# Projecting eight narrow main tiles and four 32-row strips in one go, in place of three groups on the full TensorE array

## The chip, the cores and the metric

One core of a Trainium2 chip. The metric is device microseconds (us) of one execution.

## The reference, cut to what matters

```python
B, T, D, K = (2, 16000, 144, 15)          # x: B,T,D   w: K,D,2D   w_o: D,D   all bf16
# h = causal convolution of x with 15 taps, dilation 2
f = h[..., :D].copy()
g = h[..., D:].copy()
z = jnp.tanh(f) * _sigmoid(g)
return z @ w_o
```

The last line, `z @ w_o`, is the projection. D is 144, which is 16 more than the 128 rows of the TensorE array. The change is about how those 16 are carried.

## The kernel before, as far as the change touches it

The 32,000 positions are cut into 128 segments, one for each row of the array, and time is handled in "octets": eight consecutive time steps of all 128 segments. The z of an octet has 8 x 144 = 1152 columns. One DMA transposes it into nine blocks of 128 rows, `ZT[:, zt, 0..8, :]`, each of which is the stationary operand of matmuls with w_o as the moving one. In the kernel before, the 1152 columns lie in their natural order, so most blocks hold the end of one time step and the start of the next. Blocks inside a group therefore need w_o shifted and padded with zeros for two steps (288 columns), those at a group's border for one (144 columns):

```python
GROUPS = ((0, 3), (3, 6), (6, 8))

def project(o, gi, last=False):
    a, c = GROUPS[gi]
    ...
    bk = _Bank()                                   # one PSUM bank a group
    for blk in range(a, c + 1):
        q0, q1 = max(blk - 1, a), min(blk, c - 1)
        wi = 2 * blk - 1 if q0 == blk - 1 else 2 * blk
        def f(t, q0=q0, n=q1 - q0 + 1, ...):
            c0 = bk.b * 512 + (q0 - a) * D
            return t.matmul(PS[:, c0:c0 + n * D], lhsT=ZT[:, zt, blk, :], rhs=WOR[:, wi:wi + n, :]..., start=first, ...)
        fns.append(f)
    g.add("pe", fns, r=[("ZT", zt)] + wor_keys, alloc=[bk], ...)
    # ... ScalarE evicts the bank to OS, which frees it (L847); the third group also stores OS
```

The convolution is done in 30 units, as sums of products in pairs of banks; a unit makes half of the time steps of two octets, so that on average one octet is projected in a unit. Three small pieces matter here. "Ya" (weights `WV`, two matmuls) fills one bank of a pair, and ScalarE copies that bank to the other one of the pair. "Yb" (`WD,DD`, four matmuls) then adds to both. "Xa" (`WT,DU`, two matmuls) fills the first bank of another pair, for which two banks must be free. All other large items are sums of four to eight matmuls; the "D" items, of which `D11` comes first (`WA,DD`), add to banks that VectorE has prepared.

```python
def copy(bk):      # L898 before, L924 after
    g.add("act", lambda e: e.activation(bank(bk.b + 1), bank(bk.b), ACT.Copy), w=[bk], ...)
def item_Ya(u):
    s["Y", 0] = _pair()
    shared(s["Y", 0], V..., V..., WV[:, 0, :], WV[:, 1, :], ...)   # two matmuls
    copy(s["Y", 0])
def item_Xa(u, k):
    s["X", k] = _pair()
    shared(s["X", k], DU..., DU..., WT..., WT..., ...)             # two matmuls
    copy(s["X", k])
def item_Yb(u):    # four matmuls into both banks of s["Y", 0]
    ...
    g.add("pe", fns, r=keys, w=[s["Y", 0]], dur=4 * MM)
```

The order of a unit on TensorE is a string that a list scheduler follows (O0, O1, O2 are the three groups of the projection; a plus sign marks work of the next unit or the one after it, begun early):

```python
PATTERN = "Y0a O2+ X0a+ O1+ Y0b X0b+ D11 D00 S0+ X1a+ D10 Y01 S1+ X1b+ D01 VE+ VF+ O0+"
```

After the D items, `finish` makes tanh and sigmoid on ScalarE into TS and one multiply of 288 columns on VectorE into Z.

## Time and profile before

| | before |
|---|---|
| time, median of 2 (lowest, highest) | 322.32 us (322.23, 322.41) |
| span of the profiled core | 320.3 us |
| one unit in the steady stretch | 9.37 us |
| TensorE, VectorE, ScalarE busy | 313.1, 282.5, 269.6 us |
| projection of an octet, start to start | 0.98 us |

TensorE is the engine that the others wait for, so the unit's 9.37 us is a sum of TensorE's steps. The shown durations of matmuls overlap (the last of a run is shown 0.16 us beyond its step), so steps are read from one start to the next. The lines that carry this are in the prediction below. One more is wanted for comparison later, from the waits of the kernel before; it gives an instruction, what released it, the total in us, how often, and the longest:

```profile
PEld PS L740 <- ACT PS L925: 4.3, 23, 0.4
```

It is a small wait that the kernel before already has, about 0.2 us of the weight loads' time in most units, for ScalarE's copy of the sum "S1".

### The profile page before, as it was taken

The page shows a single profiled execution, that of the slowest core. Times are in us where ns is not written, and L with a number is a line of the kernel's source. Part 1 is how long each engine was busy: PE and PEld are TensorE (multiplying, and loading weights), DVE is VectorE, ACT ScalarE, POOL GpSimd, SP SyncE. Part 2 cuts the span into 40 slices and gives each one's busy share as a digit, 9 for nine tenths or more (in the row PEclk, how much of TensorE's full clock was granted, in tenths as well). Part 3 has the DMA queues.
Part 4 walks back from the last instruction along what each step waited for, and adds up shares of the span by engine and source line. Part 5 has one row for each costly group of instructions (what it writes and reads, how often), then busy time and mean ns, then how long its engine had stood idle before and what let it go on. Part 6 is the DMA issues. An engine that isn't in the chain of part 4 may idle for free.

```text
span 320.3 us, 6963 instructions
## 1 busy us (share of the span) xinstructions
PE 313.1 (98%) x2670; PEld 243.4 (76%) x2670; DVE 282.5 (88%) x610; ACT 269.6 (84%) x636; POOL 16.9 (5%) x29
## 2 busy tenths in 40 slices
PE   7999999999999999999999999999999999999994
PEld 6877777777777777777777777777777777777674
DVE  2999989898998989899898989989898998884774
ACT  3898789889797988979798897979889797778674
POOL 8109100000000000000000000000000000000000
PEclk9999999999999999999999999999999999999999
DMA  8799994939599494978959398894949377131653
GB/s 211 228 225 202 239 194 91 202 92 207 157 145 234 86 230 103 188 171 103 281 84 242 96 200 155 141 248 77 224 120 193 89 144 170 48 69 70 113 128 96
DMA packets 127822, 50.40 MB, mean 157 GB/s; under 512 B 119134, under 2 KB 121615, under 8 KB 127789
## 3 DMA queue, kind: packets, MB, share of 16 engines
q1 hardware_dynamic: 127273, 49.62, 74.7%
q0 software_dynamic: 512, 0.33, 0.5%
q8 instruction: 21, 0.34, 0.4%
q14 instruction: 12, 0.10, 0.1%
q10 hardware_dynamic: 4, 0.01, 0.0%
HBM read 11.82 MB, written 9.22 MB: 66 GB/s over the span
## 4 chain that ended last, share of the span: by engine, by line
PE 89%; ACT 5%; DVE 2%; DMA 2%; issue 1%; POOL 0%; ACTq 0%; POOLq 0%
PE PS L740 77%; PE PS L839 9%; DMA XA<-STA 2%; PE PS L548 1%; ACT STA L652 1%; ACT STB L672 1%; ACT XA L581 1%; DVE Xp L1019 0%; ACT XB L613 0%; PE PS L572 0%; DVE DD L692 0%; ACT TS L764 0%; PE PS L870 0%; PE PS L797 0%; ACT OS L847 0%
## 5 line engine op out<-in xcount | busy, mean ns | idle before, releaser
L1019 DVE TENSOR_TENSOR Xp<-PS,UX 128x576 f32<-128x576 f32 x90 | 62.9, 751 | 19.6 <-PE PS L740 19.3
L740 PE MATMUL PS<-WB,XB 128*128 128x288 bf16 x260 | 71.9, 286 | 0.0
L1031 DVE TENSOR_TENSOR PS<-PS,Xp 128x576 f32<-128x576 f32 x90 | 68.4, 760 | 2.1 <-ACT OS L847 1.0
L740 PE MATMUL PS<-WA,GD 128*128 128x288 bf16 x360 | 69.9, 286 | 0.0
L761 ACT ACTIVATE TS<-PS 128x288 f16<-128x288 f32 x125 | 51.7, 413 | 12.2 <-PE PS L740 11.2
L847 ACT ACTIVATE OS<-PS 128x432 bf16<-128x432 f32 (+1 forms) x88 | 42.3, 488 | 13.7 <-PE PS L839 12.8
L764 ACT ACTIVATE TS<-PS 128x288 f16<-128x288 f32 x125 | 51.4, 412 | 0.0
L672 ACT ACTIVATE STB<-XBc 128x768 bf16<-128x768 bf16 x60 | 50.8, 854 | 0.5 <-DVE XBc L639 0.5
L898 ACT ACTIVATE PS<-PS 128x288 f32<-128x288 f32 x120 | 46.2, 407 | 2.6 <-PE PS L740 2.4
L967 ACT ACTIVATE UX<-PS 128x576 f32<-128x576 f32 x60 | 39.2, 654 | 10.4 <-PE PS L740 10.1
L740 PE MATMUL PS<-WS,GU 128*128 128x288 bf16 x210 | 44.3, 287 | 0.0
L839 PE MATMUL PS<-WOR,ZT 128*128 128x144 bf16 (+1 forms) x322 | 42.4, 253 | 0.0
L740 PEld LDWEIGHTS PS<-WA,GD 128*128 128x128 bf16 x360 | 34.6, 98 | 9.8 <-DVE PS L1031 0.9
L769 DVE TENSOR_TENSOR Z<-TS 128x288 bf16<-128x288 f16 x125 | 37.1, 301 | 4.3 <-ACT TS L764 4.0
L740 PE MATMUL PS<-WC,XB 128*128 128x288 bf16 x120 | 34.3, 286 | 0.0
L839 PEld LDWEIGHTS PS<-WOR,ZT 128*128 128x128 bf16 x322 | 27.9, 98 | 6.3 <-ACT OS L847 0.5
L740 PE MATMUL PS<-WD,DD 128*128 128x288 bf16 x180 | 31.9, 286 | 0.5 <-ACT PS L898 0.5
L740 PE MATMUL PS<-WC,V 128*128 128x288 bf16 x180 | 30.6, 286 | 0.0
L740 PE MATMUL PS<-WA,DD 128*128 128x288 bf16 x180 | 30.6, 286 | 0.0
L740 PEld LDWEIGHTS PS<-WB,XB 128*128 128x128 bf16 x260 | 25.4, 98 | 6.4
L740 PE MATMUL PS<-WT,DU 128*128 128x288 bf16 x120 | 24.5, 286 | 0.1
L740 PEld LDWEIGHTS PS<-WS,GU 128*128 128x128 bf16 x210 | 18.5, 98 | 7.5 <-ACT PS L898 0.3
(82 smaller groups left out, 468.6 us busy)
## 6 DMA issues: line engine op xcount, KB each, us to landing
Xr<-in_x_dram SPq DMA_DIRECT2D x15, 576.0 KB, 4.6
out_dram<-OS SPq DMA_DIRECT2D x30, 288.0 KB, 3.0
WA<-in_w_dram SPq DMA_DIRECT2D x3, 288.0 KB, 5.3
ZT<-Z SPq DMA_TRANSPOSE x32, 3.7
Xp<-in_x_dram SPq DMA_DIRECT2D x2, 252.0 KB, 5.4
XA<-STA SPq DMA_TRANSPOSE x30, 3.5
XB<-STB SPq DMA_TRANSPOSE x30, 4.8
Xp<-in_x_dram SPq DMA_DIRECT2D x1, 441.0 KB, 4.3
```

Source lines behind the costliest of these rows:

```text
L548: g.add("pe", [lambda t: t.matmul(PS[:, BANK_O * 512:BANK_O * 512 + 128], lhsT=ID[:], rhs=ONES[:], start=True, stop=True)] * n, r=["ID", " ...
L672: return v.activation(STB[:, q, 6 * h:6 * h + 6, :], src, ACT.Copy)
L740: return lambda t: t.matmul(bank(bk.b), lhsT=lhs(), rhs=rhs(), start=start, stop=True, skip_group_check=True)
L761: return a.activation(TS[:, s, 0, :, :], both(bk, 0, D), ACT.Tanh)
L764: return a.activation(TS[:, s, 1, :, :], both(bk, D, D), ACT.Sigmoid)
L769: return v.tensor_tensor(dst, TS[:, s, 0, :, :], TS[:, s, 1, :, :], ALU.mult)
L839: return t.matmul(PS[:, c0:c0 + n * D], lhsT=ZT[:, zt, blk, :], rhs=WOR[:, wi:wi + n, :].rearrange("p a b -> p (a b)"), start=first, stop= ...
L847: return e.tensor_copy(dst, src) if eng == "dve" else e.activation(dst, src, ACT.Copy)
L898: g.add("act", lambda e: e.activation(bank(bk.b + 1), bank(bk.b), ACT.Copy), w=[bk], dur=t_act(N2), prio=0)
L967: g.add("act", lambda e: e.activation(UX[:, k, u % NU, :, :], both(X, 0, N2), ACT.Copy), r=[X], w=[("UX", k, u % NU)], frees=[X], dur=t_ac ...
L1019: g.add("dve", lambda v, k=k, wi=wi, vb=vb, us=us: v.tensor_tensor(wslot(wi), both(vb, 0, N2), UX[:, k, us, :, :], ALU.add), r=[vb, ("UX", ...
L1031: return v.tensor_tensor(both(d, 0, N2), src, wslot(wi), ALU.add)
```

## The change

The intent is to save TensorE time. The 16 channels left over from each time step are put together in the ninth block: two steps fill 32 rows. Four matmuls of 288 columns, each on its own strip of 32 rows of the array, then run side by side, while the other 128 channels of each step are one matmul of 144 columns on the full array. The core of the diff, with cuts marked by dots:

```diff
-        GROUPS = ((0, 3), (3, 6), (6, 8))
-        def project(o, gi, last=False):
+        def project(o, last=False):
             zt, os_ = o % NZT, oslot(o)
-            bk = _Bank()
+            pairs = [_pair(), _pair()] if o >= 0 else [_pair()]
...
+            def main(t, q):
+                c0 = (bk_of(q // 2).b + q // 2 % 2) * 512 + q % 2 * D
+                return t.matmul(PS[:, c0:c0 + D], lhsT=ZT[:, zt, q, :], rhs=WOM[:], start=q % 2 == 0, ...)
+            def rest(t, b, r0, n):
+                c0 = (bk_of(b).b + b % 2) * 512
+                return t.matmul(PS[:, c0:c0 + 2 * D], lhsT=ZT[r0:r0 + n, zt, 8, :],
+                                rhs=WOX[r0:r0 + n, 2 * b:2 * b + 2, :]..., start=False, ...)
+            if o >= 0:
+                fns = [lambda t, q=q: main(t, q) for q in range(8)] + [lambda t, b=b: rest(t, b, 32 * b, 32) for b in range(4)]
+                dur, out = 4 * MM + MM + SWITCH, [(pairs[0], 0, 4), (pairs[1], 4, 8)]
...
+            for pb, a, c in out:       # two evictions of two banks (576 columns) each, L874
+                def ev(e, ...): ...
-    PATTERN = "Y0a O2+ X0a+ O1+ Y0b X0b+ D11 D00 S0+ X1a+ D10 Y01 S1+ X1b+ D01 VE+ VF+ O0+"
+    PATTERN = "O1 Y0a X0a+ Y0b D11 X0b+ D00 S0+ X1a+ D10 Y01 S1+ X1b+ D01 VE+ VF+"
```

Besides this: w_o is loaded in 9 DMAs and not 16; two D items' gates are multiplied together in two VectorE instructions of 512 and 64 columns (L791) and not two of 288; TS has six slots and not four; the orders of the first and last units were retuned; and in a middle unit, as the two last lines of the diff show, D11 now stands directly behind Yb and ahead of X0b, where it stood behind X0b. `SWITCH` is 0.2 us, the author's allowance for turning the array to strips and back, which only the scheduler uses.

More of the change, by code (lines that the diff above doesn't have):

```diff
@@ L361, in _conv_wavenet_kernel @@
     NO = 3
-    NTS = 4
+    NTS = 6
     NST = 2
@@ L369, in _conv_wavenet_kernel @@
     LAG = 2
-    PATTERNS = {29: 'O2 O1 Y01 Y0a D11 O0 Y0b D01 D00 D10', 28: 'Y0a X0a+ O1+ Y0b X0b+ O2+ D11 S0+ D10 X1a+ D00 Y01 S1+ X1b+ VE+ O0+ D01 VF+', 1: 'Y0a O2+ X0a+ Y0b X0b+ D11 X1a+ O1+ D00 S0+ D10 Y01 S1+ X1b+ D01 VE+ VF+ O0+', 0: 'Y0a X0a+ Y0b D11 X0b+ D00 X1a+ O2+ O1+ O0+ S0+ D10 Y01 S1+ X1b+ D01 VE+ VF+', 2: 'Y0a O2+ X0a+ O1+ Y0b X0b+ D11 D00 S0+ X1a+ D10 Y01 S1+ X1b+ D01 VE+ O0+ VF+'}
+    SWITCH = 0.2
+    PATTERNS = {29: 'O1 Y01 Y0a D11 Y0b D01 D00 D10', 28: 'X0a+ Y0a O1 Y0b X0b+ D11 S0+ D10 X1a+ D00 Y01 S1+ X1b+ VE+ D01 VF+', 1: 'Y0a O1 X0a+ Y0b X0b+ D11 X1a+ D00 S0+ D10 Y01 S1+ X1b+ D01 VE+ VF+', 0: 'Y0a O1 X0a+ X0b+ Y0b D11 D00 X1a+ S0+ D10 Y01 S1+ X1b+ D01 VE+ VF+', 2: 'O1 Y0a X0a+ Y0b D11 X0b+ D00 X1a+ S0+ D10 Y01 S1+ X1b+ D01 VE+ VF+', 27: 'O1 Y0a D11 X0a+ Y0b S0+ X0b+ D00 X1a+ D10 Y01 S1+ X1b+ D01 VE+ VF+'}
     EARLY = 4
     EARLYC = 1
-    SPREAD = 12
+    SPREAD = 11
     SPREAS = 9
-    PATTERN = "Y0a O2+ X0a+ O1+ Y0b X0b+ D11 D00 S0+ X1a+ D10 Y01 S1+ X1b+ D01 VE+ VF+ O0+"
+    PATTERN = "O1 Y0a X0a+ Y0b D11 X0b+ D00 S0+ X1a+ D10 Y01 S1+ X1b+ D01 VE+ VF+"
     with contextlib.ExitStack() as st:
@@ L397, in _conv_wavenet_kernel @@
         WB = sb("WB", [NP, 3, N2], BF16)
-        WOR = sb("WOR", [NP, 16, D], BF16)
+        WOM = sb("WOM", [NP, D], BF16)
+        WOX = sb("WOX", [NP, 8, D], BF16)
         ONES = sb("ONES", [NP, NP], BF16)
@@ L528, in _conv_wavenet_kernel @@
         g.add("pool", lambda p: p.memset(XBc[:, 4:6, MB - 1, :], 0.0), w=["XBcz"], dur=0.2)
-        g.add("pool", lambda p: p.memset(Z[:], 0.0), w=[("Z", i, d) for i in range(NZ) for d in range(8)], dur=1.2)
-        g.add("pool", lambda p: p.memset(WOR[:], 0.0), w=["WORz"], dur=1.9)
+        g.add("pool", lambda p: p.memset(Z[:], 0.0), w=[(k, i, d) for k in ("Z", "Zr") for i in range(NZ) for d in range(8)], dur=1.2)
+        g.add("pool", lambda p: p.memset(WOX[:], 0.0), w=["WORz"], dur=1.0)
         g.add("sp", ld_wb(0), w=[("WB", 0)], dur=0.5, dma="wb", nbytes=73728)
@@ L754, in zslot, with finish @@
             return (o + 2 if o > 2 * LASTP and dl % 2 else o) % NZ
-        def finish(bk, z0, z1):
+        half_done = []
+        def finish(bk, z0, z1, mode=0):
+            if mode == 1 and ts_n[0] % 2:
+                ts_n[0] += 1
             s = ts_n[0] % NTS
@@ L765, in finish, with gt @@
             op = g.add("act", [th, sg], r=[bk], w=[("TS", s)], frees=[bk], dur=2 * t_act(2 * D), prio=0)
-            def gt(v):
-                dst = bass.AP(Z[:].tensor, (z0[0] * 8 + z0[1]) * D, [[NZ * 8 * D, NP], [((z1[0] - z0[0]) * 8 + z1[1] - z0[1]) * D, 2], [1, D]])
-                return v.tensor_tensor(dst, TS[:, s, 0, :, :], TS[:, s, 1, :, :], ALU.mult)
-            g.add("dve", gt, r=[("TS", s)], w=[("Z",) + z0, ("Z",) + z1], dur=t_tt(2 * D))
+            if mode == 1:
+                half_done.append((s, z0, z1))
+                return op
+            if mode == 3:
+                def gt(v):
+                    dst = bass.AP(Z[:].tensor, z0[0] * 8 * D + (z0[1] - 1) * DA, [[NZ * 8 * D, NP], [(z1[0] - z0[0]) * 8 * D, 2], [1, D]])
+                    return v.tensor_tensor(dst, TS[:, s, 0, :, :], TS[:, s, 1, :, :], ALU.mult)
+                g.add("dve", gt, r=[("TS", s)], w=[("Z",) + z for z in (z0, z1)] + [("Z", z[0], z[1] - 1) for z in (z0, z1)], dur=t_tt(2 * D))
+                return op
+            sets = [(s, z0, z1)]
+            if mode == 2:
+                sets.insert(0, half_done.pop())
+                assert sets[0][0] == s - 1 and sets[0][1][0] == z0[0] and sets[0][2][0] == z1[0]
+            n, s0, a0, a1 = len(sets), sets[0][0], sets[0][1], sets[0][2]
+            dd = z0[1] - a0[1]
+            for c0, base, w in ((0, 0, DA), (DA, 8 * DA, DB)):
+                def gt(v, c0=c0, base=base, w=w):
+                    dst = bass.AP(Z[:].tensor, a0[0] * 8 * D + base + a0[1] * w, [[NZ * 8 * D, NP], [dd * w, n], [(a1[0] - a0[0]) * 8 * D + (a1[1] - a0[1]) * w, 2], [1, w]])
+                    src = [bass.AP(TS[:].tensor, s0 * 4 * D + q * 2 * D + c0, [[NTS * 4 * D, NP], [4 * D, n], [D, 2], [1, w]]) for q in range(2)]
+                    return v.tensor_tensor(dst, src[0], src[1], ALU.mult)
+                g.add("dve", gt, r=[("TS", x[0]) for x in sets], w=[("Z" if c0 == 0 else "Zr",) + z for x in sets for z in x[1:]], dur=t_tt(2 * n * w))
             return op
-        wor_keys = [("WORp", dl, part) for dl in range(8) for part in range(2)]
+        wor_keys = [("WOR", dl) for dl in range(-1, 8)]
         tl_n = [0]
@@ L786, in ship_pair @@
             fns = []
-            for c0, bk in ((dl * D - 112, pa), (dl * D + DB, pb)):
+            for c0, bk in (((dl - 1) * DA, pa), (dl * DA, pb)):
                 for i in range(2):
@@ L796, in ship_pair @@
                 for k in range(2):
-                    fns.append(lambda t, i=i, k=k: t.matmul(PS[:, bo.b * 512 + i * D:bo.b * 512 + i * D + D], lhsT=zt(q, 256 * k + 128 * i, 128), rhs=WOR[:, 14 + k, :],
+                    fns.append(lambda t, i=i, k=k: t.matmul(PS[:, bo.b * 512 + i * D:bo.b * 512 + i * D + D], lhsT=zt(q, 256 * k + 128 * i, 128), rhs=WOM[:] if k == 0 else WOX[:, 0, :],
                                                             start=(i == 0 and k == 0), stop=True, skip_group_check=True))
@@ L821, in ship @@
             d0 = 6 if o < 0 else 0
-            g.add("sp", lambda e: e.dma_start_transpose(ZT[:, zt, d0:9, :], Z[:, z, d0 * 128:9 * 128]), r=[("Z", z, d) for d in dls],
+            g.add("sp", lambda e: e.dma_start_transpose(ZT[:, zt, d0:9, :], Z[:, z, d0 * 128:9 * 128]), r=[(k, z, d) for k in ("Z", "Zr") for d in dls],
                   w=[("ZT", zt)], dur=1.3, dma="zt", nbytes=(9 - d0) * 32768, soft=(xb2,))
-        GROUPS = ((0, 3), (3, 6), (6, 8))
-        def project(o, gi, last=False):
-            a, c = GROUPS[gi]
-            assert o >= 0 or gi == 2
+        def project(o, last=False):
@@ L830, in project @@
             zt, os_ = o % NZT, oslot(o)
-            bk = _Bank()
+            pairs = [_pair(), _pair()] if o >= 0 else [_pair()]
+            bk_of = lambda b: pairs[b // 2 if o >= 0 else 0]
             fns = []
-            for blk in range(a, c + 1):
-                q0, q1 = max(blk - 1, a), min(blk, c - 1)
-                wi = 2 * blk - 1 if q0 == blk - 1 else 2 * blk
-                def f(t, q0=q0, n=q1 - q0 + 1, blk=blk, wi=wi, first=(blk == a)):
-                    c0 = bk.b * 512 + (q0 - a) * D
-                    return t.matmul(PS[:, c0:c0 + n * D], lhsT=ZT[:, zt, blk, :], rhs=WOR[:, wi:wi + n, :].rearrange("p a b -> p (a b)"),
-                                    start=first, stop=True, skip_group_check=True)
-                fns.append(f)
@@ L842, in project @@
-            g.add("pe", fns, r=[("ZT", zt)] + wor_keys, alloc=[bk], dur=0.1255 + 0.1227 * (c - a - 1), floating=last, prio=3 if last else 1)
-            eng = "dve" if last else "act"
-            def ev(e):
-                dst, src = OS[:, os_, a:c, :].rearrange("p e d -> p (e d)"), PS[:, bk.b * 512:bk.b * 512 + (c - a) * D]
-                return e.tensor_copy(dst, src) if eng == "dve" else e.activation(dst, src, ACT.Copy)
-            op = g.add(eng, ev,
-                       r=[bk], w=[("OS", os_, d) for d in range(a, c)], frees=[bk], dur=t_ps((c - a) * D) if last else t_act((c - a) * D), prio=2 if last else 1)
@@ L850, in project @@
-            if os_ in last_store:
-                op.deps.add(last_store[os_])
-            if gi == 2:
-                projected.add(o)
-                d0 = 6 if o < 0 else 0
-                def stf(e):
-                    dst = bass.AP(out_t, (KD + 8 * o + d0) * D, [[L * D, NP], [1, (8 - d0) * D]])
-                    return e.dma_start(dst, OS[:, os_, d0:8, :].rearrange("p e d -> p (e d)"))
-                last_store[os_] = g.add("sp", stf, r=[("OS", os_, d) for d in range(d0, 8)], w=[], dur=0.5, dma="st", nbytes=NP * (8 - d0) * D * 2)
+            def main(t, q):
+                c0 = (bk_of(q // 2).b + q // 2 % 2) * 512 + q % 2 * D
+                return t.matmul(PS[:, c0:c0 + D], lhsT=ZT[:, zt, q, :], rhs=WOM[:], start=q % 2 == 0, stop=True, skip_group_check=True)
@@ new lines, in rest @@
+            def rest(t, b, r0, n):
+                c0 = (bk_of(b).b + b % 2) * 512
+                return t.matmul(PS[:, c0:c0 + 2 * D], lhsT=ZT[r0:r0 + n, zt, 8, :], rhs=WOX[r0:r0 + n, 2 * b:2 * b + 2, :].rearrange("p a b -> p (a b)"),
+                                start=False, stop=True, skip_group_check=True)
+            if o >= 0:
+                fns = [lambda t, q=q: main(t, q) for q in range(8)] + [lambda t, b=b: rest(t, b, 32 * b, 32) for b in range(4)]
+                dur, out = 4 * MM + MM + SWITCH, [(pairs[0], 0, 4), (pairs[1], 4, 8)]
+            else:
+                fns = [lambda t, q=q: main(t, q) for q in (6, 7)] + [lambda t: rest(t, 3, 0, NP)]
+                dur, out = 2 * MM, [(pairs[0], 6, 8)]
@@ new lines, in project, with ev @@
+            g.add("pe", fns, r=[("ZT", zt)] + wor_keys, alloc=pairs, dur=dur, floating=last, prio=3 if last else 1)
+            eng = "dve" if last else "act"
+            for pb, a, c in out:
+                def ev(e, pb=pb, a=a, c=c):
+                    nb = (c - a) // 2
+                    dst = OS[:, os_, a:c, :].rearrange("p (b e) d -> p b (e d)", b=nb)
+                    src = bass.AP(PS[:].tensor, (pb.b + a % 4 // 2) * 512, [[8 * 512, NP], [512, nb], [1, 2 * D]])
+                    return e.tensor_copy(dst, src) if eng == "dve" else e.activation(dst, src, ACT.Copy)
+                op = g.add(eng, ev, r=[pb], w=[("OS", os_, d) for d in range(a, c)], frees=[pb],
+                           dur=t_ps((c - a) * D) if last else t_act((c - a) * D), prio=2 if last else 1)
+                if os_ in last_store:
+                    op.deps.add(last_store[os_])
@@ L861, in project_some, with stf @@
+            projected.add(o)
+            d0 = 6 if o < 0 else 0
+            def stf(e):
+                dst = bass.AP(out_t, (KD + 8 * o + d0) * D, [[L * D, NP], [1, (8 - d0) * D]])
+                return e.dma_start(dst, OS[:, os_, d0:8, :].rearrange("p e d -> p (e d)"))
+            last_store[os_] = g.add("sp", stf, r=[("OS", os_, d) for d in range(d0, 8)], w=[], dur=0.5, dma="st", nbytes=NP * (8 - d0) * D * 2)
         def project_some(o, dls):
@@ L869, in mk @@
                         for k in range(2):
-                            out.append(lambda t, i=i, dl=dl, k=k: t.matmul(PS[:, bk.b * 512 + i * D:bk.b * 512 + i * D + D], lhsT=ZT[:, zt, dl + k, :], rhs=WOR[:, 2 * dl + k, :],
+                            out.append(lambda t, i=i, dl=dl, k=k: t.matmul(PS[:, bk.b * 512 + i * D:bk.b * 512 + i * D + D], lhsT=ZT[:, zt, 8 if k else dl, :], rhs=WOX[:, dl, :] if k else WOM[:],
                                                                            start=(i == 0 and k == 0), stop=True, skip_group_check=True))
@@ L1062, in item_D @@
             dl = {0: 6, 1: 4, 2: 2, 3: 0}[p] + r
-            finish(bk, (zslot(o0, dl), dl), (zslot(o1, dl), dl))
+            s["nd"] = s.get("nd", 0) + 1
+            finish(bk, (zslot(o0, dl), dl), (zslot(o1, dl), dl), 3 if u == NUN - 1 else 2 - s["nd"] % 2)
         def direct(k, b, pi, t0, t1, after=None):
@@ L1141, in _conv_wavenet_kernel, with f @@
         g_diffs(-1)
-        for dl in range(8):
-            for part in range(2):
-                r0, r1, s0 = (16 * dl, 128, 0) if part == 0 else (0, 16 + 16 * dl, 128 - 16 * dl)
-                def f(e, r0_=r0, r1_=r1, s0_=s0, i_=2 * dl + part):
-                    return e.dma_start(WOR[r0_:r1_, i_, :], bass.AP(wo_t, s0_ * D, [[D, r1_ - r0_], [1, D]]))
-                op = g.add("pool", f, r=["WORz"], w=[("WORp", dl, part)], dur=0.5, dma="wor", nbytes=(r1 - r0) * D * 2)
-                op.deps.add(xb2)
+        for dl in range(-1, 8):
+            def f(e, dl=dl):
+                if dl < 0:
+                    return e.dma_start(WOM[:], bass.AP(wo_t, 0, [[D, DA], [1, D]]))
+                return e.dma_start(WOX[DB * dl:DB * dl + DB, dl, :], bass.AP(wo_t, DA * D, [[D, DB], [1, D]]))
+            op = g.add("pool", f, r=["WORz"], w=[("WOR", dl)], dur=0.5, dma="wor", nbytes=(DA if dl < 0 else DB) * D * 2)
+            op.deps.add(xb2)
         nl = [1]
@@ L1194, in _conv_wavenet_kernel @@
         reach = max(o for _, o in pattern)
-        todo = [(-1, 2, 1), (0, 0, 2), (0, 1, 2), (0, 2, 2)]
+        todo = [(-1, 1), (0, 2)]
         done_d = {}
@@ L1217, in _conv_wavenet_kernel @@
                     for _ in range(2 if t >= NUN - 3 else 1):
-                        if t >= 0 and todo and todo[0][2] <= t:
-                            project(*todo.pop(0)[:2])
+                        if t >= 0 and todo and todo[0][1] <= t:
+                            project(todo.pop(0)[0])
                     continue
@@ L1234, in _conv_wavenet_kernel @@
                             ship(o, range(8))
-                            todo += [(o, gi, t + LAG) for gi in range(3)]
+                            todo.append((o, t + LAG))
                     elif done_d[u] == 4 and u == NUN - 2:
@@ L1242, in _conv_wavenet_kernel @@
         for x in todo:
-            project(*x[:2], last=True)
+            project(x[0], last=True)
         m, r, o0, o1 = octs(NUN - 1)
```

## The prediction

> **What bounds the kernel now.** I read the engine totals first, then the steady stretch by windows, then the groups, then the timeline of one unit, and last the only place in the tail where the kernel before already does what the change will do everywhere.
>
> ```profile
> PE 313.1 (98%) x2670; PEld 243.4 (76%) x2670; DVE 282.5 (88%) x610; ACT 269.6 (84%) x636; POOL 16.9 (5%) x29
> ...
> PE 89%; ACT 5%; DVE 2%; DMA 2%; issue 1%; POOL 0%; ACTq 0%; POOLq 0%
> ```
>
> ```profile
> 91.33:100.70 9.37, 9.37 (x82) 7.27 (x80) 8.43 (x18) 8.26 (x21) 0.00 (x0) 1.00 1.12 220
> 100.70:110.08 9.38, 9.38 (x82) 7.23 (x80) 9.27 (x22) 8.39 (x21) 0.00 (x0) 1.00 0.44 112
> ```
>
> The work runs in 30 units of two blocks of eight time steps ("octets"); between about 63 and 297 us one unit takes 9.37 us. TensorE is busy for all of it (first figure after the length), VectorE for 8.43 and 9.27 us in turn (mean 8.85), ScalarE for 8.3. So TensorE sets the pace and nothing hides a microsecond added to it; VectorE is only half a microsecond behind, so even a free projection could not win more than about 0.5 us a unit.
>
> ```profile
> L839 PE MATMUL PS<-WOR,ZT 128*128 128x144 bf16 x176 | 37.7, 226 | 0.0
> L839 PE MATMUL PS<-WOR,ZT 128*128 128x288 bf16 x146 | 32.1, 286 | 0.0
> L847 ACT ACTIVATE OS<-PS 128x432 bf16<-128x432 f32 x58 | 30.4, 528 | 1.8 <-PE PS L839 1.8
> L847 ACT ACTIVATE OS<-PS 128x288 bf16<-128x288 f32 x30 | 12.3, 411 | 12.0 <-PE PS L839 11.0
> L967 ACT ACTIVATE UX<-PS 128x576 f32<-128x576 f32 x60 | 39.2, 654 | 10.4 <-PE PS L740 10.1
> L769 DVE TENSOR_TENSOR Z<-TS 128x288 bf16<-128x288 f16 x125 | 37.1, 301 | 4.3 <-ACT TS L764 4.0
> ```
>
> L839 is the projection of an octet: 6 matmuls of 144 columns and 5 of 288, in three groups of one bank each. Matmul durations overlap, so I take start-to-start steps. The 64 main matmuls of a unit take 7.89 us in the chain; without the 0.16 us by which the last outlasts its step (286 ns less a step), that is 7.73 / 63 = 0.1226 us a step. The timeline shows where the three groups stand:
>
> ```profile
> 108.44 0.41 PE L839 MATMUL PS<-WOR,ZT 128*128 128x144 bf16 x3
> 108.68 0.41 PE L740 MATMUL PS<-WV,V 128*128 128x288 bf16 x2
> 108.93 0.53 PE L839 MATMUL PS<-WOR,ZT 128*128 128x144 bf16 x4
> 109.30 0.41 PE L740 MATMUL PS<-WT,DU 128*128 128x288 bf16 x2
> 109.54 0.53 PE L839 MATMUL PS<-WOR,ZT 128*128 128x144 bf16 x4
> 109.91 0.65 PE L740 MATMUL PS<-WD,DD 128*128 128x288 bf16 x4
> ```
>
> The starts show it: 0.24 + 0.37 + 0.37 = 0.98 us of projection, with no gap. A group of four (two narrow, two wide) takes 0.37, so a narrow step is (0.37 - 2 x 0.1226) / 2 = 0.062 us. A unit has 68 other matmuls: 68 x 0.1226 + 0.98 = 9.32, which is the unit but for 0.05. What matters beside the cost is the place. The pair of matmuls on WV (call it Ya) makes a product that ScalarE must copy to a second bank before the four on WD (Yb) may add to it; the pair on WT,DU (Xa) lies between. The last two groups of the projection fill TensorE while that copy runs. Three more lines of the same unit give ScalarE's steps, and unit 28 shows what happens where nothing fills the copy:
>
> ```profile
> 106.25 0.65 ACT L925 ACTIVATE PS<-PS 128x576 f32<-128x576 f32 x1
> 106.82 0.65 ACT L967 ACTIVATE UX<-PS 128x576 f32<-128x576 f32 x1
> ...
> 108.88 0.41 ACT L847 ACTIVATE OS<-PS 128x288 bf16<-128x288 f32 x1
> ```
>
>
> ```profile
> 297.36 0.41 PE L740 MATMUL PS<-WV,V 128*128 128x288 bf16 x2
> 297.60 0.41 PE L740 MATMUL PS<-WT,DU 128*128 128x288 bf16 x2
> 298.50 0.66 PE L740 MATMUL PS<-WD,DD 128*128 128x288 bf16 x4 [0.49 <-ACT PS L898]
> ...
> 297.31 0.83 ACT L847 ACTIVATE OS<-PS 128x432 bf16<-128x432 f32 x2 [1.13 <-PE PS L839]
> 298.03 0.72 ACT L898 ACTIVATE PS<-PS 128x288 f32<-128x288 f32 x2
> ```
>
> There the projection stood before Ya; ScalarE evicted it first (L847), the copy (L898) queued behind, and TensorE showed 0.49 us idle.
>
> **What the Trainium skill says.** "TensorE: Matmul & The Clock Gate", Part 3, gives row strips as concurrent: the span of n strips is one matmul plus about 4 ns for each further one. "TensorEngine Tiling (Array Packing)", Key Properties, says that a change of tiling mode, not just of tile, drains TensorE; it gives no time. The kernel before uses the full array alone, so its trace says nothing on either. "PSUM — Partial Sum Buffer", Specifications, gives 8 banks; that is what the kernel shares out, and the new projection wants four of them at once. The table at the head of the first page calls ScalarE's queue strict FIFO; the trace agrees: at 297.31 and 298.03 above the copy waits behind the evictions.
>
> **The change part by part.** In the built program an octet has eight narrow matmuls (full array, 128 channels), then four of 288 columns on 32-row strips, in four banks.
>
> TensorE, matmuls: 8 x 0.062 = 0.50; the four strips together one step of 0.1226 and 3 x 0.004 = 0.135. That would be 0.63 against 0.98, 0.35 saved. I add one drain before the strips. As an estimate I take what a 288-column matmul lasts beyond its step, 286 - 123 = 163 ns, because the strips' weights may have to wait for an empty array. That gives 0.80 us, and 0.18 saved. The drain back costs nothing extra, for the next paragraph's reason.
>
> TensorE, waits: this is the part that decides. The built order of a middle unit is projection, Ya, Xa, Yb, with nothing between, and this sequence stands 25 times. One signal follows the last strip, so both evictions start only then; each now covers two banks (576 columns). All eight banks are taken: four by the projection, two by Ya, two by the sums of the previous phase (VF). So Xa waits for the first eviction, and Yb for Ya's copy, which ScalarE has in its order after that eviction. From the end E of the projection's stream, with the trace's durations:
> - the strips' result is complete at E + 0.16, ScalarE starts 0.03 later (108.44 + 0.41 = 108.85 to 108.88 above) at E + 0.19 and lasts 0.65 (L967 has this size); with 0.05 from ScalarE to TensorE (L925 ends at 106.90, the matmul that waited for it starts at 106.95), Xa starts at E + 0.90. Ya has used 0.245 of that: idle 0.65;
> - the next ScalarE instruction starts 0.57 after a 576-column one (L925 to L967 in the same unit), so the copy starts at E + 0.76, lasts 0.41, and Yb starts at E + 1.22; Xa has ended its stream at E + 1.145: idle another 0.08.
> So 0.73 us of idle where there was none. Whatever the drain back costs, Ya still ends long before E + 0.90. Net for a unit: 0.73 - 0.18 = +0.55, a period of 9.92. 25 x 0.55 = 13.8 us.
>
> The ends: twice (units 27 and 29) two whole projections follow each other; the second needs a bank pair of the first and waits about 0.9 us for its eviction, less 2 x 0.18 saved each time: about +1 us in both. Setup: nine loads of w_o instead of 16, on an idle queue: 0.
>
> ScalarE: evictions fall from 58 x 0.528 + 30 x 0.411 = 43.0 to 58 x 0.654 + 0.41 = 38.3 us, 4.7 less; off the path, except as the latency above. VectorE: two multiplies of 301 ns become one of 512 columns and one of 64. Such subtractions take 419 ns at 512 and 684 at 1024 columns, so 0.52 ns a column on 154 ns: 419 + 187 = 606 against 602. It is neutral, but comes in one burst between the adds that the D matmuls wait for. With the longer period these adds are early enough.
>
> Sum: 322.3 + 13.8 + 1.0 = 337.1; I take off half a microsecond for the unit's 0.05 us of old waits, part of which should vanish: 336.5 us.
>
> **The rivals.**
> 1. The strips are nearly free and TensorE's saving comes through: 29 x 0.35 = 10 us, VectorE then capping it: about 313. For it: TensorE carries 89% of the chain, and the author retuned the order for this layout. Against: bank and copy waits are fixed in the program, and each is a lower bound.
> 2. The author's own allowance for the switch (0.2 us, in the diff) is right and the waits hide: 29 x (0.98 - 0.82) = 4.6 us, 317.7, within 2%. Against: the 0.49 us gap in unit 28.
> 3. The switch costs far more than a drain, the weights of four strips load one after the other: 0.3 us more an octet, 8 to 9 us on top: 345.
> 4. VectorE's bursts become the bound: 8.85 us of 9.9 leaves it a tenth idle; I expect under 1 us from it.
>
> **Range and chances.** The waits have little spread (0.65 to 0.8). The projection itself can be 0.63 to 1.0 us, so the net per unit is +0.38 to +0.77: 9.5 to 19 us for 25 units, 332 to 342 with the ends. Range 331.5 to 342. Slower by over 2% means over 328.8, which even the free switch passes: 0.89. Within 2%: 0.08, if an idle I count overlaps something. Faster: 0.03, only if I have misread the order.
>
> **What would show it.** Unit length near 9.9, not 9.37 or less. Before Xa an idle of 0.5 to 0.65 us named after ScalarE's eviction, 25 times, and a short one before Yb after the copy (shown idle is up to 0.16 smaller than the true one, as shown ends overlap the next step). Start of the first narrow matmul to start of Ya: 0.80 if one drain, 0.63 if none, over 1.0 if weights queue. The multiply pair 0.6 us. Wrong would be: no idle before Xa; a unit shorter than 9.5; or new idle in front of the D matmuls, released by VectorE.

## The result, and the profile after

| | before | after |
|---|---|---|
| time, median of 2 (lowest, highest) | 322.32 (322.23, 322.41) | 337.75 us (337.31, 338.18) |
| span of the profiled core | 320.3 | 335.6 us |
| one unit (25 units from unit 2 on, by the start of each unit's first `WC,GV` matmul) | 234.25 / 25 = 9.370 | 247.79 / 25 = 9.912 us |

The ratio is 1.0457, with a 95% interval from 1.0415 to 1.0499: slower. Ratios here and below are the mean time of one kernel's fast runs over that of the other's of the same rounds, so they are not quite the ratio of the medians quoted.

The engine totals and the chain of waits of the changed kernel:

```profile
PE 316.5 (94%) x2699; PEld 233.8 (70%) x2699; DVE 283.0 (84%) x615; ACT 269.6 (80%) x607; POOL 12.0 (4%) x22
...
PE 89%; ACT 9%; issue 1%; DVE 0%; POOL 0%; ACTq 0%; POOLq 0%
```

TensorE is now busy for 94% and no longer 98%, and ScalarE's share of the chain that ended last rose from 5% to 9%: ScalarE is not busier (269.6 us in both), but TensorE waits for it. Two units of the steady stretch by windows (length, then busy time of PE, PEld, DVE, ACT and POOL, granted clock, DMA share, GB/s):

```profile
113.68:123.65 9.97, 9.57 (x80) 6.89 (x81) 8.51 (x18) 8.40 (x20) 0.00 (x0) 1.00 1.08 226
123.65:133.50 9.85, 9.45 (x80) 6.96 (x81) 9.11 (x21) 8.29 (x20) 0.00 (x0) 1.00 0.39 86
```

Before, the first two figures were equal; now 0.40 us of each unit shows no matmul at all (more in truth, by the overlap). The timeline of one unit, TensorE's and ScalarE's rows at the place of the change:

```profile
112.02 0.66 PE L855 MATMUL PS<-WOM,ZT 128*128 128x144 bf16 x8
112.62 0.30 PE L859 MATMUL PS<-WOX,ZT 32*128 32x288 bf16 x4
112.85 0.42 PE L742 MATMUL PS<-WV,V 128*128 128x288 bf16 x2
112.97 0.65 ACT L874 ACTIVATE OS<-PS 128x576 bf16<-128x576 f32 x1 [0.59 <-PE PS L859]
113.52 0.41 ACT L924 ACTIVATE PS<-PS 128x288 f32<-128x288 f32 x1
...
113.68 0.42 PE L742 MATMUL PS<-WT,DU 128*128 128x288 bf16 x2 [0.41 <-ACT OS L874]
...
113.98 0.66 PE L742 MATMUL PS<-WD,DD 128*128 128x288 bf16 x4
```

Read it from the first row as zero. The strips start at 0.60, Ya at 0.83, the first eviction at 0.95, Ya's copy at 1.50, Xa at 1.66 and Yb at 1.96. In the kernel before, projection, Ya and Xa are all through in 0.98 + 2 x 0.245 = 1.47, the copy having run beside them. Here Yb starts half a microsecond later. The idle before Xa is named after the eviction L874. The waits add it up over the whole kernel:

```profile
PEld PS L742 <- ACT OS L874: 18.5, 26, 0.7
...
PE PS L742 <- ACT OS L874: 10.6, 26, 0.4
...
PEld PS L742 <- ACT PS L951: 5.8, 24, 0.4
```

There are 26 such stops in 30 units. (The first row is the weight load's wait for the same event, longer because loads run ahead.) The third row is the counterpart of the wait shown for the kernel before, 4.3 us there; it grew a little. The evictions and multiplies by form:

```profile
L874 ACT ACTIVATE OS<-PS 128x576 bf16<-128x576 f32 x58 | 37.2, 647 | 28.0 <-PE PS L859 28.0
...
L791 DVE TENSOR_TENSOR Z<-TS 128x512 bf16<-128x512 f16 x58 | 24.3, 419 | 7.2 <-ACT TS L770 7.2
...
L791 DVE TENSOR_TENSOR Z<-TS 128x64 bf16<-128x64 f16 x58 | 10.6, 183 | 0.0
```

### The profile page after: what moved, and what is told of

Its sections match the earlier page's. It is cut to its first block, busy times and chain, and to the rows that moved or that the text cites. A ratio compares the mean times of both kernels' runs of the same rounds, so it can differ in the third digit from the quotient of the medians.

```text
span 335.6 us, 7011 instructions
## 1 busy us (share of the span) xinstructions
PE 316.5 (94%) x2699; PEld 233.8 (70%) x2699; DVE 283.0 (84%) x615; ACT 269.6 (80%) x607; POOL 12.0 (4%) x22
## 4 chain that ended last, share of the span: by engine, by line
PE 89%; ACT 9%; issue 1%; DVE 0%; POOL 0%; ACTq 0%; POOLq 0%
PE PS L742 80%; ACT OS L874 6%; PE PS L855 4%; PE PS L859 2%; PE PS L550 1%; ACT TS L767 1%; ACT PS L924 1%; PE PS L574 1%; ACT TS L770 0%; ACT OS L823 0%; PE PS L819 0%; ACT STB L674 0%; ACT Xr L814 0%; PE PS L611 0%; ACT PS L951 0%
## 5 line engine op out<-in xcount | busy, mean ns | idle before, releaser
L874 ACT ACTIVATE OS<-PS 128x576 bf16<-128x576 f32 (+1 forms) x59 | 37.6, 643 | 28.0 <-PE PS L859 28.0
L791 DVE TENSOR_TENSOR Z<-TS 128x512 bf16<-128x512 f16 (+1 forms) x126 | 34.6, 296 | 7.3 <-ACT TS L770 7.2
L742 PEld LDWEIGHTS PS<-WS,GU 128*128 128x128 bf16 x210 | 20.4, 98 | 5.6 <-ACT PS L924 0.5
L694 DVE TENSOR_TENSOR V<-XA 128x1024 bf16<-128x1024 bf16 (+2 forms) x39 | 23.4, 610 | 0.0
L742 PEld LDWEIGHTS PS<-WT,DU 128*128 128x128 bf16 x120 | 9.0, 97 | 20.5 <-ACT OS L874 17.8
```

The costliest lines, as they stand in the source:

```text
L694: return g.add("dve", lambda v: v.tensor_tensor(dst, a, b, ALU.subtract), r=r, w=wk, dur=t_tt(n), prio=prio, soft=gate[:1])
L742: return lambda t: t.matmul(bank(bk.b), lhsT=lhs(), rhs=rhs(), start=start, stop=True, skip_group_check=True)
L791: return v.tensor_tensor(dst, src[0], src[1], ALU.mult)
L874: return e.tensor_copy(dst, src) if eng == "dve" else e.activation(dst, src, ACT.Copy)
```

## The experiments

The theory: the strips work as meant and their switches cost about what the author allowed; what costs is the gathering of the projection in four banks at one place, since then Xa waits for a late eviction and Yb for a copy queued behind it. The rivals: the switch to strips and back is the cost; the strips do not run side by side; VectorE's larger multiplies are the cost. Nine kernels were run. Those that give a wrong result are marked. Times are medians of 4 runs (6 in the last), beside a kernel before that was between 322.67 and 322.80 us in the same jobs.

### 1. The same gathering, wide matmuls on the full array

```diff
- ... + [lambda t, b=b: rest(t, b, 32 * b, 32) for b in range(4)]
+ ... + [lambda t, b=b: rest(t, b, 0, NP) for b in range(4)]
```

No strip and no switch is left; everything else is the changed kernel. The result is right, as the other rows of the weights are zero.

> Changed kernel with the four strips replaced by four full-array matmuls of 288 columns (the rows outside the strip are zero in the weights, so the result stays right); same order, same waits, no switch of tiling mode. Wait theory (after the last matmul of the projection the first eviction, then the copy of Ya, hold TensorE): the projection's result comes at 0.50 + 4 x 0.1226 = 0.99 us of stream instead of the 0.74 seen (112.02 to 112.92 less 0.16), so +0.25 us in each of 27 places: about +6.8, 344.5 us. Rival 1 (the switch of the array's mode is what costs the time): without strips the loss goes, about 322 or less. Rival 2 (the new layout of Z and the pairwise multiplies on VectorE cost it): 337, no change.

Measured: 344.82 us, ratio 1.0676 (1.0651 to 1.0702). The timeline of a unit:

```profile
114.29 0.66 PE L855 MATMUL PS<-WOM,ZT 128*128 128x144 bf16 x8
114.79 0.65 PE L859 MATMUL PS<-WOX,ZT 128*128 128x288 bf16 x4
115.28 0.41 PE L742 MATMUL PS<-WV,V 128*128 128x288 bf16 x2
```

Eight narrow matmuls take 0.50 and four wide ones 0.49, where the changed kernel has 0.60 and 0.23. So the first switch costs 0.10 us, and the strips still save 0.16 of the stream. Their result is complete 0.24 us sooner counted to the eviction (1.19 us after the first row here, 0.95 there): they end together, and the switch back comes after them. A unit is 10.155 us and not 9.92, the same 0.24. The strips are worth 7 us where they stand. The rival that they or their switches are the loss falls.

### 2. No leftover matmuls at all (wrong result)

```diff
- for q in range(8)] + [lambda t, b=b: rest(t, b, 32 * b, 32) for b in range(4)]
+ for q in range(8)]
```

> Changed kernel with the strips left out altogether (wrong result on purpose): the eight full-array matmuls alone, same order and waits. Wait theory: result at 0.50 us of stream instead of 0.74, -0.24 x 27 = -6.5, so 331 us: still some 9 us slower than before although TensorE then does 29 x 0.48 = 14 us less matmul work than before. Rival 1 (mode switch): below 322, towards 322 - 14 = 308. Rival 2 (VectorE): about 337.

Measured: 335.61 us, ratio 1.0387 (1.0355 to 1.0419); relative error 0.33, as intended. It is a miss: 2 us came off and not 7. Even a projection without strips and without a switch is 4% slower than the kernel before, which speaks for the theory; but something else stands right behind the two waits. The timeline shows it:

```profile
112.26 0.66 PE L855 MATMUL PS<-WOM,ZT 128*128 128x144 bf16 x8
...
113.96 0.67 PE L742 MATMUL PS<-WD,DD 128*128 128x288 bf16 x4
...
114.62 0.24 PEld L742 LDWEIGHTS PS<-WA,DD 128*128 128x128 bf16 x3 [0.31 <-DVE PS L1066]
```

Yb starts 1.70 us after the first row, 0.26 sooner than in the changed kernel, as expected. But D11, the next item, waits for an add of VectorE (L1066) and starts at 114.63, 2.37 after the first row and only 0.09 sooner (114.48 - 112.02 = 2.46 there). VectorE does three adds, then the 512-column multiply of the change, and only then that add.

### 3. The strips twice (wrong result)

```diff
- [lambda t, b=b: rest(t, b, 32 * b, 32) for b in range(4)]
+ [lambda t, b=b: rest(t, b, 32 * b, 32) for b in range(4)] * 2
```

> Changed kernel with the four strips issued twice in a row (wrong result on purpose), no further switch. If the strips do run side by side, a second pass costs one 288-column step and three small ones, 0.135 us, all of it ahead of the eviction: 27 x 0.135 = +3.6, 341.4 us. If they ran one after the other, 4 x 0.1226 = 0.49: +13, 351 us. If the time around the strips is mostly mode switch, the pass costs the 0.135 all the same.

Measured: 341.25 us, ratio 1.0568 (1.0540 to 1.0597).

```profile
113.96 0.42 PE L859 MATMUL PS<-WOX,ZT 32*128 32x288 bf16 x8
114.32 0.42 PE L742 MATMUL PS<-WV,V 128*128 128x288 bf16 x2
```

Eight strips take 0.36 us and four take 0.23 with the same switch. A pass of four is thus 0.13 us, the step of a single full matmul; the other 0.10 of the 0.23 is the switch back. The rival that the strips run one after another falls: that would be 0.49 a pass. The changed kernel's own trace agrees: one strip matmul lasts 292 ns (L859, by form), and all four together are shown for 0.30 us (the row at 112.62 above), so they start within about 0.01 us of each other.

### 4. The kernel before with its three groups gathered

```diff
-    PATTERN = "Y0a O2+ X0a+ O1+ Y0b X0b+ D11 D00 S0+ X1a+ D10 Y01 S1+ X1b+ D01 VE+ VF+ O0+"
+    PATTERN = "O0 O2 O1 Y0a X0a+ Y0b X0b+ D11 D00 S0+ X1a+ D10 Y01 S1+ X1b+ D01 VE+ VF+"
```

This is the gathering alone: the same matmuls as before, the same three banks and evictions, the same multiplies.

> Kernel before with nothing changed but the place of its three projection groups in the middle units: all three ahead of Ya instead of one before Ya, one between Ya and Xa and one between Xa and Yb. No strips, no new layout, the same instructions. Wait theory: ScalarE evicts the three groups (0.43 + 0.43 + 0.31 us of its time) before it copies Ya's product, Xa waits for the second eviction and Yb for the copy; from the groups' start to Yb 2.19 us by the durations in the trace, of which 0.98 + 0.49 is work: 0.72 us of idle in each of 25 units, +18, 340 us. Rivals 1 and 2: 322, as nothing of theirs is in it.

Measured: 343.81 us, ratio 1.0656 (1.0619 to 1.0693), 21 us more than the kernel before from a change of order alone.

```profile
112.84 1.15 PE L839 MATMUL PS<-WOR,ZT 128*128 128x144 bf16 x11
...
114.41 0.42 PE L740 MATMUL PS<-WT,DU 128*128 128x288 bf16 x2 [0.18 <-ACT OS L847]
...
115.02 0.66 PE L740 MATMUL PS<-WD,DD 128*128 128x288 bf16 x4 [0.19 <-ACT PS L898]
```

Yb starts 2.18 us after the first row, where 2.19 was expected. Both waits are there, with the same names. The time is 4 us above what was expected, since in every other unit a further wait for ScalarE's tanh and sigmoid appears; units take 10.07 and 10.45 us in turn.

### 5. No leftover matmuls, the multiply behind the add (wrong result)

Experiment 2, and on VectorE the 512-column multiply is put behind the add that it stood before:

```diff
+        vo = g.order["dve"]
+        for i in range(1, len(vo)):
+            if vo[i] in adds and vo[i - 1] in muls:
+                vo[i - 1], vo[i] = vo[i], vo[i - 1]
```

> The run without strips again (wrong result on purpose), with one thing more: on VectorE the 512-column multiply is put behind the add that the next D matmuls (WA,DD) wait for. Theory of two limits, formed on the miss of the run without strips: behind the eviction wait stands a second one, three adds, the multiply and the fourth add on VectorE, which let these matmuls start 2.37 us after the projection's first one, where the changed kernel had 2.46; so only 0.09 could be won. Without the multiply in between the add ends 0.34 earlier, and the matmuls start at 1.70 + 0.49 = 2.19: 25 x 0.27 = -6.7 from 337.75, 331 us (against 335.6 with the multiply in its place). If the miss had another cause: no change, 335.6.

Measured: 333.53 us, ratio 1.0335 (1.0304 to 1.0367). D11 now starts 2.21 us after the projection does (111.15 to 113.36; 2.19 expected) and no longer 2.37, so the multiply was the second limit. But only 2 of the 4.6 us came: the waits now list 6.8 us, in 24 places, for a later add of VectorE (L1059), which comes after the moved multiply in its queue. That the move pushed it back is likely, as the same add held TensorE up only 3 times (0.9 us) in experiment 2, but it was not tested by itself. VectorE is busy for 8.8 us of each unit in the kernel before and in the changed one, so there is little room to move work on it.

### 6. The new layout in four groups of one bank, on the full array

The eight main matmuls are split in four groups of two, each with one full-array matmul of 288 columns for its leftover channels and one eviction, and put back into the places of the kernel before. In short:

```diff
-        def project(o, last=False):
+        def project(o, gi, last=False):
+            bk = _Bank()
-            fns = [main q for q in range(8)] + [rest(t, b, 32 * b, 32) for b in range(4)]
+            fns = [main q for q in (2 * gi, 2 * gi + 1)] + [rest(t, 0, NP)]
-    PATTERN = "O1 Y0a X0a+ Y0b D11 X0b+ D00 S0+ X1a+ D10 Y01 S1+ X1b+ D01 VE+ VF+"
+    PATTERN = "Y0a O2+ X0a+ O1+ O3+ Y0b X0b+ D11 D00 S0+ X1a+ D10 Y01 S1+ X1b+ D01 VE+ VF+ O0+"
```

> Layout, pairwise multiplies and six TS buffers of the change kept, but the projection issued in four single-bank groups (two narrow matmuls and one full-array 288) which stand among the other matmuls as the three groups of the kernel before did; no strips, no gathering. Theory: the layout and the multiplies cost nothing. The matmul work is what it was (0.99 us an octet); by the waits in the built program the fourth group waits for the eviction of the second, about 0.17 us a unit: 322 to 327 us. Rival 2 (multiply bursts on VectorE, 8.85 us of a unit of 9.4): near 337.

Measured: 331.07 us, ratio 1.0265 (1.0234 to 1.0296); a miss. The fourth group needs a bank that an eviction frees late:

```profile
PEld PS L852 <- ACT OS L863: 10.3, 27, 0.5
```

```profile
101.64 0.29 PE L852 MATMUL PS<-WOM,ZT 128*128 128x144 bf16 x2
101.77 0.29 PE L855 MATMUL PS<-WOX,ZT 128*128 128x288 bf16 x1
102.20 0.30 PE L852 MATMUL PS<-WOM,ZT 128*128 128x144 bf16 x2
```

The group before it ends its stream at 101.89 (101.77 and a step) and this one starts at 102.20: 0.31 us, 27 times, 8.4 us, which is the whole loss against the kernel before. On ScalarE Ya's copy stands before the eviction in question. So a fourth bank for the projection, with its group directly behind the third, is by itself enough to bring such a wait back.

### 7. The same four groups, each wide matmul on its own strip

```diff
- rest(t, 0, NP)
+ rest(t, 32 * gi, 32)
```

> The four single-bank groups, with the 288-column matmul of each on its own 32-row strip, so eight switches of tiling mode an octet instead of two and none of them side by side. From the changed kernel's trace (eight narrow matmuls of 0.50 took 0.60 to the first strip, strips to Ya 0.23 against 0.135) a switch costs about 0.1 us: 4 x 0.2 = 0.8 a unit on top of the run with full matmuls, less what its 0.17 of waiting absorbs: +18 to +23 us. If a switch is a full drain of 0.16 and the loading of weights, 0.3 each: +65.

Measured: 346.01 us, ratio 1.0722 (1.0691 to 1.0753), 14.9 us over experiment 6. With one strip at a time nothing can run side by side, so only the switches are seen:

```profile
103.70 0.29 PE L852 MATMUL PS<-WOM,ZT 128*128 128x144 bf16 x2
103.92 0.29 PE L855 MATMUL PS<-WOX,ZT 32*128 32x288 bf16 x1
104.15 0.42 PE L742 MATMUL PS<-WV,V 128*128 128x288 bf16 x2
```

0.22 and 0.23 us, where full-array steps take 0.125 and 0.123: a switch is 0.10 us in each direction. Four pairs of 0.2 us are 0.8 a unit; the 0.31 us wait of experiment 6 has gone into them, and 0.49 x 29 = 14.3 us is left, near the 14.9 measured. My range missed because it left that wait in.

### 8. The strips first, and a signal after the first half

The strips go first (with `start=True`), then the main matmuls 0 to 3 with a signal for the first eviction, then 4 to 7; the multiply is moved as in experiment 5. The result is right.

```diff
- fns = [main q for q in range(8)] + [strips]
+ fns = [strips] + [main q for q in range(4)]
+ g.add("pe", [main q for q in range(4, 8)], r=..., w=[pairs[1]], ...)
```

> Changed kernel with the strips ahead of the eight full-array matmuls, and a signal after the first four of these, so that the eviction of the first bank pair starts 0.25 us earlier relative to the projection's end; and the multiply behind the add, as in the run without strips. Same matmuls and result. Wait theory: first pair done at 0.585 + 0.166 = 0.75 us, Xa at 1.48, Yb at 1.81, D matmuls at 2.30 instead of 2.46: 25 x 0.16 = -4, about 333.7 us. Rival 1: 337.75, the switches being the same. It can't reach the kernel before: 0.83 us of projection and some 0.2 of waiting left against 0.98.

Measured: 335.57 us, ratio 1.0401 (1.0363 to 1.0439). The rows that carry the reading:

```profile
111.84 0.29 PE L742 MATMUL PS<-WA,V 128*128 128x288 bf16 x1
112.06 0.30 PE L861 MATMUL PS<-WOX,ZT 32*128 32x288 bf16 x4
...
112.75 0.65 ACT L878 ACTIVATE OS<-PS 128x576 bf16<-128x576 f32 x1 [0.43 <-PE PS L857]
...
114.26 0.53 PE L742 MATMUL PS<-WA,DD 128*128 128x288 bf16 x3
```

Here the first switch comes before the projection's first matmul: the matmul before it starts at 111.84 and its step ends at 111.96. Counted from there, as the changed kernel is, the first eviction starts at 0.79 and no longer at 0.95, and D11 at 2.30 and no longer at 2.46, just where the expectation had it. The unit is shorter by less than those 0.16 us, 9.80 against 9.91 us, and about half of the 4 us expected is lost. The waits point to VectorE again: weight loads wait 3.0 us, in 11 places, for its adds (L1061), and 0.8 us, in 3 places, in the changed kernel. It is the fastest correct form of the gathered projection that I ran, by 2 us, and still 4% slower than the kernel before.

### 9. The new layout in the three groups of before, on the full array

Groups of 3, 3 and 2 time steps, with one full-array matmul of 432 or 288 columns for the leftover channels, in the places and orders of the kernel before. Layout, loads, multiplies and buffers are those of the change.

```diff
-        def project(o, last=False):
+        def project(o, gi, last=False):
+            a, c = ((0, 3), (3, 6), (6, 8))[gi]
+            bk = _Bank()
-            fns = [main q for q in range(8)] + [rest(t, b, 32 * b, 32) for b in range(4)]
+            fns = [main q for q in range(a, c)] + [rest(t, 0, NP)]
-    PATTERN = "O1 Y0a X0a+ Y0b D11 X0b+ D00 S0+ X1a+ D10 Y01 S1+ X1b+ D01 VE+ VF+"
+    PATTERN = "Y0a O2+ X0a+ O1+ Y0b X0b+ D11 D00 S0+ X1a+ D10 Y01 S1+ X1b+ D01 VE+ VF+ O0+"
```

> Everything of the change but the strips and the gathering: layout of Z, pairwise multiplies, six TS buffers, w_o in two tiles; the projection in three single-bank groups (3, 3 and 2 narrow matmuls and one wide full-array matmul of 432, 432 and 288 columns: 0.98 us as before) in the very places of the kernel before. The run with four groups lost 0.31 us a unit (102.20 instead of 101.89) to one more eviction wait, which this has not. Theory: the layout and the multiplies cost nothing, 322 to 323.5 us. Rival 2 (multiply bursts on VectorE hold the D matmuls): the 8 us that the run with four groups showed over the kernel before stay, about 330.

Measured over five rounds: 324.68 us (6 runs, 324.12 to 325.26), ratio 1.0051 (1.0014 to 1.0087). A unit is 9.44 us, 0.07 over the kernel before. The waits point to where from:

```profile
PEld PS L742 <- DVE PS L1047: 7.6, 37, 0.5
```

These are waits for adds on VectorE; the kernel before has 0.9 us of them, in 4 places, and experiment 6 has 0.5 us, in one place, perhaps because its longer units give VectorE more time; this was not tested. So the paired multiplies and the layout together cost about half a per cent, slightly more than I expected, and nothing like 15 us.

### The sum of it

By ratios to the kernel before: the layout with its multiplies is +0.0051 (experiment 9); gathering it in four banks adds 0.0625 (experiment 1 less 9); the strips give back 0.0219 (the change less experiment 1). That is +1.6, +20.1 and -7.1 us on 322.3, together +14.7 (the medians of the first job differ by 15.4). The step from 9 to 1 also changes the number of banks, the orders of the first and last units and the place of D11 in the middle ones, so "gathering" here means all of that, and as experiment 6 shows no loss for the layout beside its wait, the parts need not add up in any other combination; experiment 4 shows that the gathering of the old matmuls alone has the same size, 21 us.

## Why the prediction was right, point by point

**TensorE's matmuls.** The prediction had 0.50 for the mains, 0.135 for the strips and one visible drain of 0.16: 0.80 us. Measured is 0.83, by another make-up: 0.50 + 0.13 and two switches of 0.10 each, both visible in the stream of matmuls (experiments 1, 3 and 7). Part of the agreement is luck: one drain of 0.16 stood for two switches of 0.10. Taking 163 ns for a drain, the shown overhang of a matmul, was too much for one. That the switch back "costs nothing extra" held in the sense that counts: it delays Ya, but neither the strips' result nor, with it, the eviction and Xa.

**The wait before Xa and Yb.** This was the deciding step, and it held. By the prediction's hand sum Xa starts 0.80 + 0.90 = 1.70 us after the projection does, and Yb at 0.80 + 1.22 = 2.02; measured are 1.66 and 1.96. The idle shown before Xa is 0.41, with the 0.16 of overlap 0.57, inside the 0.5 to 0.65 named, 26 times and not 25. The short one before Yb is seen at the weight load alone.

**The unit and the sum.** Predicted 9.92 us a unit and 13.8 us in 25 of them; measured 9.912, and 247.79 - 234.25 = 13.5 us. So two small errors cancelled here: Yb comes 0.06 sooner than the hand sum, and the rest of the unit takes about 0.06 more than before (9.91 less 1.96 against 9.37 less 1.47). There the old wait for the copy of S1, of which "part should vanish", did not: it rose from 4.3 to 5.8 us. The half microsecond taken off for it had the wrong sign.

**The ends.** Predicted +1.0 us. Measured: 51.06 against 50.72 us to the start of unit 2, +0.34, and 335.6 - 298.85 = 36.75 against 320.3 - 284.97 = 35.33 us from unit 27 to the end, +1.42. The wait that it named is there: main matmuls stand idle for an eviction twice, 1.5 us in all (the waits list `PE PS L855 <- ACT OS L874: 1.5, 2, 0.8`). But the term was mis-sized by 0.8 us; with the half microsecond, and less the 0.3 by which the 25 units came in lower, that is 1.0 of the 1.25 us between 336.5 and 337.75, and the rest is no more than the runs of one kernel differ. Which other parts of the retuned ends cost it was not tested.

**ScalarE and VectorE.** The evictions fell to 37.6 us (38.3 predicted, 42.7 before) and that bought nothing. The multiplies are 419 + 183 = 602 ns for two of 301 before, as predicted (606). "With the longer period these adds are early enough" held for the changed kernel, where weight loads wait for these adds 0.8 us in all, but with 0.09 us to spare and no more. I did not see this limit, and it made experiments 2, 5 and 8 miss: of the 6.5 us that experiment 2 should have brought, 2.1 came. Part of this limit may come from the change's own order, which puts D11 ahead of X0b: X0b's six matmuls would give VectorE's add 0.74 us more. The gathered strips were not run with X0b first, so this stays open.

**The rivals.** The first (strips free, 313 us) fails on the waits. The second has the author's 0.2 us for both switches right to the hundredth, and 0.83 against 0.98 is a true saving of 0.15 us an octet; it fails because the waits do not hide. The third (0.3 us more for the switch) fails on experiments 1 and 7. The fourth (VectorE the bound) is not the cause here but the next one in line.

**Is there a version that beats both?** None was found. The strips save much only if all four run together: by the measured steps, an estimate for two halves of two strips, with the 0.13 of a pass for each, is 0.50 + 2 x 0.13 + 4 x 0.10 = 1.16 us, more than the 0.98 of before. In this program each of the four writes a bank of its own. So the saving came with a result spread over four banks that is complete at one time, and it was that which cost more than it saved. Whether some other order of the unit could hide one long eviction stays open; experiment 8 is the nearest try.

## What to carry to other kernels

Where several small pieces of work each fill the time of somebody else's copy, merging them into one cheaper piece removes the filling as well as the work: look at what runs beside each piece before counting what the merger saves. Work out when the merged piece's buffers come free, from its last instruction through the eviction to the first item that wants a buffer, and put that beside the saving; here 0.64 us of waits (1.96 from the projection's start to Yb, less 0.83 of projection and 0.49 of Ya and Xa) stood against 0.15 saved. And when a wait is shortened and the time hardly moves, look at the next item's releaser: a second engine may have been a tenth of a microsecond behind all along.

## What the Trainium skill lacked or had wrong

- "TensorEngine Tiling (Array Packing)", Key Properties, says that a change of tiling mode drains the array and gives no time. Here it took 0.10 us from full array to 32-row strips and 0.10 us back, with matmuls of 144 and 288 columns around it (0.60 against 0.50; 0.22 and 0.23 against 0.125 and 0.123 us).
- "TensorE: Matmul & The Clock Gate", Part 3, was right: with its 4 ns spacing the estimate for a pass of four strips was 0.135 us, and a second pass added 0.13 us. What it lacks for a kernel whose matmuls are otherwise full-array is that the gain needs enough strips per switch: one strip per switch made a step of 0.12 us one of 0.22 and added 14.9 us to the whole time.
- "TensorEngine Tiling (Array Packing)" does say, under Gotcha 1, that row tiles write to different PSUM banks and so raise the pressure on PSUM, and under PSUM Bottleneck that emptying PSUM may become the limit. What the page lacks is a size. Here four of the eight banks fell due at one moment, the next item waited 0.41 us (shown) for the first eviction 26 times, and the kernel with the cheaper projection was 4.6% slower.
